# Fused attention and two expert layers: q and k of seven head pairs read by feature, key sums all on TensorE, a new written order

## The chip, the cores and the metric

The kernel runs on one core of a Trainium2 chip. The time is device microseconds (us) from the first to the last instruction of a launch, with what lies around it. Before the change the median of three runs is 609.99 us (609.46 to 610.15).

## The reference

Three layers follow one another; the change touches the first alone.

```
q_rot, k_rot = rotate(q), rotate(k)          # (2, 8, 576, 64): x1*cos - x2*sin | x1*sin + x2*cos
scores = (q_rot @ k_rot.T) / sqrt(64); scores -= max over keys
attn = exp(scores); attn /= sum over keys + 1e-9
x = attn @ v                                 # to (1152, 512)
x = leaky(x @ w_in) @ w_out                  # 512 -> 2048 -> 512
top-2 of 8 experts by noisy logits; out += gate * (relu(x @ w1[e]) @ w2[e])
```

All is computed to float32 accuracy: an operand of a product is cut into a rounded high part and a rest (low part), and a product is high·high + low·high + high·low, three TensorE passes at one pass each.

## The kernel before

Attention takes two heads (a pair) at a time, eight pairs in all, with the 576 tokens in five blocks of 128 columns (the last is half empty; the two heads share it). For each pair:

- **Loads.** SyncE's queue loads q and k by token (`load_qk`, L268: tokens on the partitions, 256 KB in rows of 1 KB and a rest of 32 KB in rows of 256 bytes) and v (`load_v`).
- **Rotation.** `rope` (L299) multiplies by cosine and sine tables and adds: four instructions for q and four for k, on VectorE for pair 0 (letter O of the order below), on GpSimd for pairs 1 to 7 (letter P).
- **Turning.** `turn` (L324; letters Q and K) makes TensorE transpose the rotated tokens into a PSUM tile, features on the partitions; ten small products for q and ten for k. The PSUM tile is one of three slots that the scores and the maxima use too.
- **High and low part.** ScalarE copies the turned tile, rounded, to `high` (`turn_high`, L349; h, i), VectorE subtracts it from the turned tile to `low` (`turn_low`, L354; j, n).
- **Maxima.** `max_scores` (M) makes plain products, VectorE reduces them (`max_reduce`, D), `max_turn` (R) and `max_rows` (m) bring the row maxima in place.
- **Scores.** `scores` (L411; S) makes a cell of 288 queries and 128 keys for both heads: four terms of two products, each product on 64 rows of TensorE's array. ScalarE takes the exponential from PSUM into `prob` (W).
- **Values and sums.** `values` (L426; V) multiplies `prob` with v on column strips of 32, four strips beside each other. `sums_of` (L444; G) multiplies with ones, in the same strips, to sum over keys. Before, key blocks 0 and 1 are added first by VectorE and blocks 2 and 3 by GpSimd (`add`, L439; + and ^), so a pair has three groups of sums: `GROUPS, ADDERS = ((0, 1), (2, 3), (4,)), ((0,), (1,))`.
- **Closing.** The sums go to DRAM and back spread over the partitions (t, T, s, B), GpSimd multiplies (N), ScalarE and GpSimd write the high and low part of x (X, Y).

What order the four compute engines and SyncE work in is written out by hand as a string `ORDER` (L508): one letter is one step, each engine takes its own steps in the string's order, and an engine that waits holds back all that stands behind it on that engine. Letter o is an idle product on TensorE; w, Z, F, l, k, c load; !, #, $, %, & and * are six steps that convert the first weights of the next layer.

`raw[pr % 2]` holds the loaded q and k of two pairs at a time. After attention the next layers run on TensorE without a gap; they aren't touched.

Of the kernel before, what the change touches and what calls it, by code (L numbers as in the profile page):

```python
# [16 lines left out]
OP = mybir.AluOpType  # L17
# [68 lines left out]
def fused_kernel(ctx, tc, q, k, v, w_in, w_out, w_gate, w_noise, noise, w1, w2, consts, out):  # L86
# [147 lines left out]
    GROUPS, ADDERS = ((0, 1), (2, 3), (4,)), ((0,), (1,))  # L234
# [12 lines left out]
    for i in range(2):  # L247
        raw.append({n: ap.tile([128, 2, KT, D], F32, name=f"raw_{n}{i}") for n in "qk"})
        VF.append(ap.tile([128, 2, 4, D], F32, name=f"VF{i}"))
        VT.append(ap.tile([128, 2, D], F32, name=f"VT{i}"))  # L250
        peak.append(ap.tile([128, KT, 65], F32R, name=f"peak{i}"))
        MR.append(ap.tile([128, KT * 128], F32R, name=f"MR{i}"))

    def fill(n):
        for t, v in ((raw[0]["q"][64:128, :, 4, :], 0.0), (raw[0]["k"][64:128, 0, 4, :], 0.0), (raw[0]["k"][0:64, 1, 4, :], 0.0),
                     (ones, 0.0), (ones[0:1, 0, :], 1.0), (ones[64:65, 0, :], 1.0), (ones[0:1, 1, 0:64], 1.0),
                     (ones[64:65, 1, 64:128], 1.0), (MR[0], 0.0), (peak[0], 0.0), 
                     (add_up[:, 0], 1.0), (add_up[0:64, 1], 1.0), (add_up[64:128, 1], 0.0), (add_up[0:64, 2], 0.0),
                     (add_up[64:128, 2], 1.0), (VT[0][64:128, 0], 0.0), (VT[0][0:64, 1], 0.0),
                     (raw[1]["q"][64:128, :, 4, :], 0.0), (raw[1]["k"][64:128, 0, 4, :], 0.0),  # L260
                     (raw[1]["k"][0:64, 1, 4, :], 0.0), (MR[1], 0.0), (peak[1], 0.0),
                     (VT[1][64:128, 0], 0.0), (VT[1][0:64, 1], 0.0))[FILLS[n][0]:FILLS[n][1]]:
            G.memset(f32(t) if t.dtype == F32R else t, v)

    FILLS = ((0, 8), (8, 10), (10, 17), (17, 24))

    def load_qk(pr, n, part, a=slice(0, 2), queue=None):

        b, h0 = divmod(pr, 4)
        h0 *= 2  # L270
        src, t = q if n == "q" else k, raw[pr % 2][n]
        base = src.offset + (b * H + h0 + a.start) * S * D
        heads = [S * D, a.stop - a.start]
        if part == 0:
            (queue or nc.sync).dma_start(t[:, a, 0:4, :].rearrange("p h j d -> p h (j d)"),
                                         bass.AP(tensor=src.tensor, offset=base, ap=[[4 * D, 128], heads, [1, 4 * D]]))
        else:
            r = 64 if n == "k" and a.start == 1 else 0
            (queue or nc.sync).dma_start(t[r:r + 64, a, 4, :],
                                         bass.AP(tensor=src.tensor, offset=base + 512 * D, ap=[[D, 64], heads, [1, D]]))  # L280
# [17 lines left out]
    def rope(pr, n, eng, i, a0=0, a1=2):  # L298
        x = raw[pr % 2][n]  # L299
        if (pr, n) not in roped:  # L300
            roped[pr, n] = [a2.tile([128, KT, 2, D], F32, name=m) for m in ("rope_" + n, "rope_t")]
        hs = slice(a0, a1)
        r, t = (y[:, :, hs] for y in roped[pr, n])
        rv, tv = (y.rearrange("p j h d -> p h j d") for y in (r, t))
        if (pr, n, i) == (1, "q", 0) and not FIRST_G:
            G.tensor_copy(hold, roped[0, "k"][0][0:1, 0, 1, 0:1])
# [16 lines left out]
    def turn(pr, n, a, at=None):  # L323


        r = roped[pr, n][0]
        if pr == 0:
            if at is None:
                p = aside.append(ps_o.tile([128, 1024], F32, name="pT", tag="o")) or aside[0]
            else:  # L330
                p = ps(at, "pT", (128, 1024))
            turned[pr, n, a] = p
            for j in range(KT):
                if a == 0:
                    T.transpose(p[:64, j * 128:(j + 1) * 128], r[:, j, 0], ident)
                else:
                    T.transpose(p[:, j * 128:(j + 1) * 128], r[:, j].rearrange("p h d -> p (h d)"), ident)
            return
        p = ps(at, "pT")
        for j in range(KT):  # L340
# [98 lines left out]
    def add(pr, g, z, eng):  # L439
        t = joined[pr, g, z] = a2.tile([128, 2, 288], F32, name=f"both{g}{z}", bufs=1)  # L440
        i, j = GROUPS[g]
        eng.tensor_tensor(t, prob[pr, i, z], prob[pr, j, z], op=OP.add)

    def sums_of(pr, g):  # L444

        y, js = acc[pr], GROUPS[g]
        for o in range(2):
            x = joined[pr, g, o] if len(js) == 2 else prob[pr, js[0], o]
            for a in range(2):
                for c in range(2):  # L450
                    T.matmul(y[64 * a + 32 * c:64 * a + 32 * c + 32, o, 288:432], add_up[:, 0 if js[0] < 4 else 1 + a],
                             x[:, a, c * 144:c * 144 + 144], start=False, stop=(g == len(GROUPS) - 1), skip_group_check=True)
# [56 lines left out]
"ckfcokcokkofokkokfokoooOoIoOfoOooOOQ0OlOoohOloOK1lOOoloiOoOlQ2OOlM0hOM1lDPKwjM0ioloDPM2woDM1lPoFDM0PoolDoooDoP"  # L509
"lQ2nR1whM0ooFPmojowS1PD!wM2oWwDPS0lM1WS2DPS0Wl+K1lWM2lViDPVF!nM0S2PDM1WPVDM2R0DM1mPlM0DS2ZDM1lWPDM0S2PDM1WVPDM"  # L510
"0S2DS1W^l+K0WlQ2M1hVDPVijVGn^M1S2DM0WVPJDR1PM2#mGGDPM0S1DM2WDS0PQ1$WS2hVPWVjM0wUPS2DwM1PWlDS0lM2WS1DPZK0+WtS2M"
"1WV+wVi^lVDlVnM2S1PDM0WVPDS2PJM1M0WDVVD^M2R1DM0mVDPM2S1DS0WTQ2PWsM1GDPhGVPjM0S1DM2PWDS0K1WM2GPDiVPnS0US2PM1WtV"
"DWV#lM0S1JDlS2W+S0lWS1+lWM2^wVDWlG!lM0R1PDM2lmVTlDS0PwS1$WsS2PWM0wVWBD^S1%S2WM0BVWPVDlM1S2DZS0PW+K1M2iVGNWnGVD"
"VPQ0UPM1S2DhPtVJVWjM1&wS2^DwS0W+ZR1WVPlmM2wS0DS1WTS2P%WM0VWPVDM1S2PDM0WVDM1NS2DM0WVD^Q1*K2hM0VXDGPiGjVXVnPM0wS"
"1PDM2FWGPDsS0UJF+M1S2wWVYZWVDtR0M2^M1mDVV!BDM0S2DlS1W+S0lW^M2VD&VWM1YS2DS0W#M1GWPDVM2S0DPS1W#Q2WPM0VDhGPVjM1S0"
"DNS2WTS1J+sWK0wWS2*i^VGWnwS1UB$S2M0!VwW%VZVWDtVX+VFM1M2R0DNwVmDZV&M1^S0DS2WTS1$sWYM0GXVWDS2S1+WS0BW+M2VW*GGDV#"
"S1%UM0S2DWtVNWV!M1M0M2^D&VVDXV^DVVTJ$VsYGFS1wS0*wWR2wW%GBVm#V$&GS1U*S0%S2WtWVWS1NS0WS2&YS1WTV+sWVFVW*V^+S0S2WB"
"S1W^GXFVVWYVGGVVNUXtY")
# [7 lines left out]
    first = [(0, n, i, slice(a, a + 1), x) for a, x in enumerate((nc.sync, nc.scalar)) for n in "qk" for i in range(2)]  # L526
# [3 lines left out]
    def idle():  # L530
# [12 lines left out]
            "O": (rope, [(0, n, V, i, a, a + 1) for n, a in FIRST_V for i in range(4)] +
                  [(pr, n, V, i) for pr, n in pairs[2:] if (pr, n) in ROPE_V for i in range(4)]),
            "P": (rope, [(0, n, G, i, a, a + 1) for n, a in FIRST_G for i in range(4)] +
                  [(pr, n, G, i) for pr, n in pairs[2:] if (pr, n) not in ROPE_V for i in range(4)]),
            "Q": (turn, [(0, "q", 0), (0, "q", 1)] + [(pr, "q", None) for pr in some]),
            "K": (turn, [(0, "k", 0), (0, "k", 1)] + [(pr, "k", None) for pr in some]),
# [16 lines left out]
    work["G"] = (sums_of, [(pr, g) for pr in range(NP) for g in range(len(GROUPS))])  # L565
# [825 lines left out]
```

## Time and profile before

| | |
|---|---|
| median of three runs | 609.99 us |
| the profiled execution | 609.47 us, its span 607.7 us |
| TensorE busy | 595.4 us, 98% |
| VectorE, ScalarE, GpSimd busy | 70%, 49%, 42% |
| attention, first instruction to the next layer's first product | 0 to 148.8 us |
| first score (S) of pair 0 | 17.23 us |
| granted clock | 0.998 |

The profile names engines PE (TensorE matrix products), PEld (its weight loads), DVE (VectorE), ACT (ScalarE), POOL (GpSimd) and SP (SyncE). Products follow one another before the one ahead has ended, so the step from one start to the next is what a product costs, and a busy PE may still be one that waits a little.

### The profile page before, as it was taken

The page shows a single profiled execution, that of the slowest core. Times are in us where ns is not written, and L with a number is a line of the kernel's source. Part 1 is how long each engine was busy: PE and PEld are TensorE (multiplying, and loading weights), DVE is VectorE, ACT ScalarE, POOL GpSimd, SP SyncE. Part 2 cuts the span into 40 slices and gives each one's busy share as a digit, 9 for nine tenths or more (in the row PEclk, how much of TensorE's full clock was granted, in tenths as well). Part 3 has the DMA queues.
Part 4 walks back from the last instruction along what each step waited for, and adds up shares of the span by engine and source line. Part 5 has one row for each costly group of instructions (what it writes and reads, how often), then busy time and mean ns, then how long its engine had stood idle before and what let it go on. Part 6 is the DMA issues. An engine that isn't in the chain of part 4 may idle for free. (4 is left out here: it accounts for less than half of the span.)

```text
span 607.7 us, 12491 instructions
## 1 busy us (share of the span) xinstructions
PE 595.4 (98%) x4736; PEld 501.4 (83%) x4737; DVE 427.3 (70%) x900; ACT 295.9 (49%) x604; POOL 254.3 (42%) x256
## 2 busy tenths in 40 slices
PE   8999999999999999999999999999999999999994
PEld 4666766777888888888999988888888888888883
DVE  7888887883898888833378667777676777776610
ACT  2554665756554544433234453454545455555411
POOL 6999799637300000100000204473838383838212
PEclk9999999999999999999999999999999999999999
DMA  6520323233357843650654431558585767676323
GB/s 194 157 54 24 109 54 112 78 86 102 97 147 264 274 139 109 222 174 2 207 171 140 151 100 48 192 178 220 155 211 180 188 189 196 181 204 181 77 39 45
DMA packets 83214, 85.84 MB, mean 141 GB/s; under 512 B 12365, under 2 KB 64973, under 8 KB 83150
## 3 DMA queue, kind: packets, MB, share of 16 engines
q1 hardware_dynamic: 76878, 73.82, 39.2%
q0 software_dynamic: 5392, 10.49, 9.1%
q8 instruction: 38, 0.62, 0.4%
q10 hardware_dynamic: 880, 0.69, 0.4%
q14 instruction: 26, 0.21, 0.1%
HBM read 69.96 MB, written 14.98 MB: 140 GB/s over the span
## 5 line engine op out<-in xcount | busy, mean ns | idle before, releaser
L968 POOL DMA_INDIRECT got<-x_rows,chunks x70 | 81.6, 1166 | 78.9 <-ACT wh L217 45.3
L219 DVE TENSOR_TENSOR wl<-raw,wh 128x512 fp32r<-128x512 f32 x128 | 82.6, 683 | 14.8 <-ACT wh L217 14.7
L599 PE MATMUL bank<-xe_h,wl 128*128 128x320 f32 x248 | 76.8, 310 | 0.0
L599 PE MATMUL bank<-xe_l,wh 128*128 128x320 f32 x248 | 76.8, 310 | 0.0
L599 PE MATMUL bank<-xe_h,wh 128*128 128x320 f32 x248 | 76.7, 309 | 0.0
L217 ACT ACTIVATE wh<-raw 128x512 fp32r<-128x512 f32 x128 | 74.2, 627 | 0.0
L620 ACT ACTIVATE g_t<-bank 128x512 f32<-128x512 f32 (+2 forms) x48 | 23.6, 492 | 94.8 <-PE bank L599 93.8
L422 ACT ACTIVATE p<-pS 128x576 f32<-128x576 f32 x80 | 49.1, 651 | 40.1 <-PE pS L418 39.0
L1160 PE MATMUL bank<-wh,g_x 128*128 128x512 f32 x192 | 68.0, 395 | 0.0
L608 PE MATMUL bank<-g_h,wh 128*128 128x512 f32 (+2 forms) x192 | 65.1, 339 | 0.0
L599 PE MATMUL bank<-xh,wh 128*128 128x512 f32 (+2 forms) x192 | 65.0, 338 | 0.0
L599 PE MATMUL bank<-xh,wl 128*128 128x512 f32 (+2 forms) x192 | 64.9, 338 | 0.0
L608 PE MATMUL bank<-g_l,wh 128*128 128x512 f32 (+2 forms) x192 | 64.7, 337 | 0.0
L599 PE MATMUL bank<-xl,wh 128*128 128x512 f32 (+2 forms) x192 | 64.7, 337 | 0.0
L608 PE MATMUL bank<-g_h,wl 128*128 128x512 f32 (+2 forms) x192 | 64.5, 336 | 0.0
L381 DVE TENSOR_REDUCE half<-pM 128x2 f32<-128x640 f32 x70 | 51.5, 754 | 16.1 <-PE pM L369 15.6
L621 DVE TENSOR_TENSOR g_f<-bank,g_t 128x512 f32<-128x512 f32 (+2 forms) x48 | 26.7, 557 | 45.4 <-ACT g_t L620 44.9
L1186 POOL DMA_INDIRECT out<-y_row,idx x24 | 39.9, 1663 | 35.7 <-ACT y_row L1171 17.9
L1141 ACT ACTIVATE g_x<-bank 128x320 fp32r<-128x320 f32 x48 | 21.0, 438 | 63.0 <-PE bank L599 59.3
L599 PEld LDWEIGHTS bank<-xe_h,wh 128*128 128x128 f32 x248 | 46.7, 188 | 5.8
L1143 DVE SCALAR_TENSOR_TENSOR g_x<-bank,g_x 128x320 fp32r<-128x320 f32 x48 | 23.4, 488 | 36.5 <-ACT g_x L1142 36.5
L599 PEld LDWEIGHTS bank<-xe_h,wl 128*128 128x128 f32 x248 | 46.6, 188 | 2.8
(250 smaller groups left out, 1436.0 us busy)
## 6 DMA issues: line engine op xcount, KB each, us to landing
raw<-in_moe_w SPq DMA_DIRECT2D x128, 256.0 KB
raw<-in_moe_w_in SPq DMA_DIRECT2D x16, 512.0 KB
raw<-in_moe_w_out SPq DMA_DIRECT2D x16, 512.0 KB
inv_sum<-inv_sums SPq DMA_DIRECT2D x16, 144.0 KB
out<-none SPq DMA_DIRECT2D x9, 256.0 KB
VF<-in_v SPq DMA_DIRECT2D x8, 256.0 KB
kept<-wh SPq DMA_DIRECT2D x4, 512.0 KB
kept<-wl SPq DMA_DIRECT2D x4, 512.0 KB
```

Source lines behind the costliest of these rows:

```text
L217: A.activation(hi[:, part], t, AF.Copy)
L219: V.tensor_tensor(lo[:, part], t, f32(hi)[:, part], op=OP.subtract)
L381: V.tensor_reduce(halves[pr, i][:, :, j], p[:, :, :(320, 256)[i]], axis=AX.X, op=OP.max, negate=True)
L422: A.activation(t, scored.pop((pr, j, z))[:, :, 0:288], AF.Exp, scale=0.125)
L599: T.matmul(h[:, :n], w[:, 0, k * 128:(k + 1) * 128], m[:, k, cols:cols + n], start=(i == 0), stop=(i == 11))
L608: T.matmul(b[:, o:o + n], w[:, 1, ds], m[:, :n], start=(first and opens and t == 0), stop=(last and t == 2), skip_group_check=True)
L620: A.activation(t[:, :n], h[:, :n], AF.Copy, scale=0.01)
L621: V.tensor_tensor(g[:, :n], h[:, :n], t[:, :n], op=OP.max)
L968: G.indirect_dma_start(out=got[e][:, b * 128:(b + 1) * 128], out_offset=None, in_=x1_rows.rearrange("n (q c) -> (n q) c", q=4), in_offset= ...
L1143: V.scalar_tensor_tensor(g[:, C:2 * C], h[:, :C], 0.0, f32(g)[:, :C], op0=OP.max, op1=OP.subtract)
L1160: T.matmul(yr[st], s, w, start=(f == 0 and t == 0), stop=(f == 7 and t == 2))
L1186: s = G.indirect_dma_start(out=out, out_offset=bass.IndirectOffsetOnAxis(ap=idx[e][:r.shape[0], st:st + 1], axis=0), in_=r, in_offset=None ...
```

## The change

- For pairs 1 to 7, q and k come from a new array `heads` that is laid out before the launch: features of both heads on the 128 partitions, tokens along the columns, once as they are and once with the two halves of the features swapped, with zeros in the empty columns. A load is 640 KB in rows of 5 KB (128 partitions x 1280 numbers). `angles` (2 x 320 KB) holds the cosines and the signed sines in the same layout.
- GpSimd rotates in place with three instructions of 640 columns for q and three for k (two products, one sum). There is no turning for these pairs: `high` and `low` are taken from `raw` in SBUF.
- Pair 0 is loaded, rotated and turned as before.
- GpSimd's additions of key blocks 2 and 3 go; TensorE sums each of these blocks by itself, four groups for a pair. The order of a pair's groups is set by `SUMS`.
- `ORDER` is another string. In it 140 of 160 turning products are gone (18 steps Q and K become 4), the 16 steps ^ are gone, G has 32 steps for 24, P 42 for 56, o 31 for 35, l 14 for 35; the other counts are the same.

```diff
+def angles():
+    ...
+    c = np.stack([np.concatenate([cos[s], cos[s]], 1), np.concatenate([-sin[s], sin[s]], 1)]).transpose(2, 0, 1)
+    return np.ascontiguousarray(np.concatenate([c, c]))
+def heads(q, k):
+    out = np.zeros((2, B * H // 2 - 1, 2, D, 2, KT * 128), np.float32)
+    for i, x in enumerate((q, k)):
+        x = np.asarray(x).reshape(B * H // 2, 2, S, D)[1:].transpose(0, 1, 3, 2)
+        for w, y in enumerate((x, np.roll(x, D // 2, axis=2))):
+            ...
-    GROUPS, ADDERS = ((0, 1), (2, 3), (4,)), ((0,), (1,))
+    GROUPS, ADDERS = ((0, 1), (2,), (3,), (4,)), ((0,), ())
+    SUMS = [(i // 4, int(g)) for i, g in enumerate("10231023012310230123102310231023")]
...
-        raw.append({n: ap.tile([128, 2, KT, D], F32, name=f"raw_{n}{i}") for n in "qk"})
+        raw.append({n: ap.tile([128, 2, KT * 128], F32, name=f"raw_{n}{i}") for n in "qk"})
+    angle = ap.tile([128, 2, KT * 128], F32, name="angle")
...
+    def load_turned(pr, n):
+        nc.sync.dma_start(raw[pr % 2][n].rearrange("p w n -> p (w n)"), heads["qk".index(n), pr - 1].rearrange("p w n -> p (w n)"))
+    def load_angle(i):
+        nc.sync.dma_start(angle[:, i], angles[:, i])
...
+    def rope_turned(pr, n, i):
+        x = raw[pr % 2][n]
+        if (pr, n, i) == (1, "q", 0) and not FIRST_G:
+            G.tensor_copy(hold, roped["k"][0][0:1, 0, 1, 0:1])
+        if i < 2:
+            G.tensor_tensor(x[:, i], x[:, i], angle[:, i], op=OP.mult)
+        else:
+            G.tensor_tensor(x[:, 0], x[:, 0], x[:, 1], op=OP.add)
...
-        for j in range(KT):
-            for w in range(2):
-                T.transpose(p[:, w, j * 64:(j + 1) * 64], r[here(w), j].rearrange("p h d -> p (h d)"), ident[here(w), here(w)])
+    def source(pr, n, a=1):
+        return raw[pr % 2][n][:, 0] if pr else turned[n, a][:, :KT * 128]
     def turn_high(pr, n, a):
-        ...
+        A.activation(high[n][pr % NSET][here(a)], source(pr, n, a)[here(a)], AF.Copy)
     def turn_low(pr, n):
-        ...
+        V.tensor_tensor(low[n][pr % NSET], source(pr, n), f32(high[n][pr % NSET]), op=OP.subtract)
...
     ORDER = (
-"ckfcokcokkofokkokfokoooOoIoOfoOooOOQ0OlOoohOloOK1lOOoloiOoOlQ2OOlM0hOM1lDPKwjM0ioloDPM2woDM1lPoFDM0PoolDoooDoP"
-"lQ2nR1whM0ooFPmojowS1PD!wM2oWwDPS0lM1WS2DPS0Wl+K1lWM2lViDPVF!nM0S2PDM1WPVDM2R0DM1mPlM0DS2ZDM1lWPDM0S2PDM1WVPDM"
...
+"ckfkokcokkookkoceokoloeoOoooOoOoOooOIQ0OfOoOohOfK1OOoofiOwoOQ2wOOM0whOM1DlKZPDM0iooFDM1ZDM0PZoDM1ZoDwM0PowjR1o"
+"womnooPloDS2FM1lWS0PDM2WS1DS0WPM2hVDVW+VPiS1M2M0WDR1PDM2mDM0S1PDM2WVDS0jPM1M2WS0DVWlPDZhM1M0VZDGPDM2S1DS0WJVi+"
...
```

## Rows read from the trace of the kernel before

**Rows 1.** The page's first part: busy us, share of the span, instructions.

```profile
PE 595.4 (98%) x4736; PEld 501.4 (83%) x4737; DVE 427.3 (70%) x900; ACT 295.9 (49%) x604; POOL 254.3 (42%) x256
```

**Rows 2.** Busy time by stretch: stretch, length, then each engine, clock, DMA share, GB/s.

```profile
0.00:17.20 17.20, 15.14 (x84) 7.97 (x85) 12.14 (x30) 5.23 (x9) 12.07 (x37) 1.00 0.69 197
17.20:83.20 66.00, 64.15 (x954) 45.12 (x955) 56.74 (x77) 37.53 (x60) 60.48 (x48) 1.00 0.29 80
83.20:148.80 65.60, 65.33 (x1067) 45.65 (x1063) 49.53 (x72) 40.18 (x68) 45.94 (x35) 1.00 0.32 89
```

**Rows 3.** TensorE's timeline, 102 to 108 us: start, length, line, tiles, count.

```profile
103.90 0.70 PE L451 MATMUL pO<-both,add_up 128*32 128x144 f32 x16
104.41 0.67 PE L435 MATMUL pO<-p,VF 128*32 128x288 f32 x8
105.01 0.39 PE L369 MATMUL pM<-high_k,high_q 64*128 64x256 f32 x2
105.23 0.30 PE L418 MATMUL pS<-high_q,high_k 64*128 64x288 f32 x2
...
106.30 0.51 PE L342 MATMUL pT<-ct,rope_q 64*128 64x64 f32 x10
106.67 0.41 PE L369 MATMUL pM<-high_k,high_q 64*128 64x320 f32 x2
```

**Rows 4.** GpSimd's timeline, 28 to 39 us.

```profile
28.79 1.56 POOL L313 TENSOR_TENSOR rope_k<-rope_k,rope_t 128x640 f32<-128x640 f32 x1
30.30 2.01 POOL L442 TENSOR_TENSOR both<-p 128x576 f32<-128x576 f32 x1
...
37.13 1.56 POOL L313 TENSOR_TENSOR rope_q<-rope_q,rope_t 128x640 f32<-128x640 f32 x1
```

**Rows 5.** TensorE's timeline, 38 to 43 us, with idle time and who ended it.

```profile
38.98 0.47 PE L342 MATMUL pT<-ct,rope_q 64*128 64x64 f32 x10
39.26 0.38 PE L418 MATMUL pS<-high_q,high_k 64*128 64x288 f32 x2
...
42.56 0.41 PE L369 MATMUL pM<-high_k,high_q 64*128 64x320 f32 x2 [0.58 <-DVE low_q L356]
```

**Rows 6.** VectorE's timeline from the first maximum to the first score.

```profile
10.35 0.76 DVE L376 TENSOR_REDUCE peak<-pM 128x1 fp32r<-128x576 f32 x1
11.03 0.81 DVE L356 TENSOR_TENSOR low_q<-pT,high_q 128x640 fp32r<-128x640 f32 x1
11.76 3.45 DVE L376 TENSOR_REDUCE peak<-pM 128x1 fp32r<-128x576 f32 x5
15.61 0.82 DVE L356 TENSOR_TENSOR low_k<-pT,high_k 128x640 fp32r<-128x640 f32 x1 [0.39 <-PE pT L532]
```

**Rows 7.** TensorE's timeline, the same stretch.

```profile
15.49 0.52 PE L342 MATMUL pT<-ct,rope_q 64*128 64x64 f32 x10
15.82 0.34 PE L396 MATMUL pR<-ident_r,peak 64*65 64x64 f32 x6
...
17.23 0.40 PE L418 MATMUL pS<-high_q,high_k 64*128 64x288 f32 x2
```

**Rows 8.** Line 442 and line 356: count, duration ns min/median/max, first and last start.

```profile
L442 DVE TENSOR_TENSOR both<-p x16: 686/752/2106, 20.3 to 142.1; 128x576 f32<-128x576 f32 x16
...
L356 DVE TENSOR_TENSOR low_q<-pT,high_q x8: 808/815/825, 11.0 to 107.9; 128x640 fp32r<-128x640 f32 x8
```

**Rows 9.** GpSimd's groups, 0 to 148 us: count, busy us, mean ns, idle before.

```profile
L442 POOL TENSOR_TENSOR both<-p 128x576 f32<-128x576 f32 x16 | 24.2, 1520 | 6.2 <-ACT p L422 6.2
L311 POOL TENSOR_TENSOR rope_t<-raw_q,ct_att 128x320 f32<-128x320 f32 x14 | 12.6, 917 | 0.0
L308 POOL TENSOR_TENSOR rope_q<-raw_q,ct_att 128x640 f32<-128x640 f32 x7 | 10.9, 1555 | 0.1
```

**Rows 10.** VectorE's additions of line 442, as groups, 0 to 148 us.

```profile
L442 DVE TENSOR_TENSOR both<-p 128x576 f32<-128x576 f32 x16 | 16.4, 1033 | 0.2 <-ACT p L422 0.2
```

**Rows 11.** Busy time by stretch, 10 to 15 us, columns as in rows 2.

```profile
10.00:15.00 5.00, 4.67 (x25) 2.77 (x25) 5.00 (x8) 1.22 (x2) 4.43 (x5) 1.00 0.86 253
```

More of the change, by code (lines that the diff above doesn't have):

```diff
@@ L78, in constants @@
     return c
+def angles():
+    half = D // 2
+    inv_freq = 1.0 / 10000.0 ** (np.arange(0, half, dtype=np.float32) / half)
+    freqs = np.outer(np.arange(S, dtype=np.float32), inv_freq)
+    cos, sin = np.cos(freqs).astype(np.float32), np.sin(freqs).astype(np.float32)
+    s = np.concatenate([(4 * np.arange(128)[None] + np.arange(4)[:, None]).reshape(-1), 512 + np.arange(128) % 64])
+    c = np.stack([np.concatenate([cos[s], cos[s]], 1), np.concatenate([-sin[s], sin[s]], 1)]).transpose(2, 0, 1)
[5 more added lines that the diff above has]
+        for w, y in enumerate((x, np.roll(x, D // 2, axis=2))):
+            out[i, :, :, :, w, :512] = y[..., :512].reshape(*y.shape[:3], 128, 4).swapaxes(3, 4).reshape(*y.shape[:3], 512)
+            for a in range(2):
+                o = 512 + 64 * a * i
+                out[i, :, a, :, w, o:o + 64] = y[:, a, :, 512:]
+    return out.reshape(2, B * H // 2 - 1, 128, 2, KT * 128)
 def f32(t):
@@ L85, in fused_kernel @@
 @with_exitstack
-def fused_kernel(ctx, tc, q, k, v, w_in, w_out, w_gate, w_noise, noise, w1, w2, consts, out):
+def fused_kernel(ctx, tc, q, k, v, w_in, w_out, w_gate, w_noise, noise, w1, w2, consts, heads, angles, out):
     nc = tc.nc
@@ L296, in fused_kernel, with rope @@
     roped = {}
[L298 to L301, printed above, removed]
+    def rope(n, eng, i, a0, a1):
+        x = first_raw[n]
+        if n not in roped:
+            roped[n] = [a2.tile([128, KT, 2, D], F32, name="rope_" + n, bufs=1), a2.tile([128, KT, 2, D], F32, name="rope_t")]
         hs = slice(a0, a1)
-        r, t = (y[:, :, hs] for y in roped[pr, n])
+        r, t = (y[:, :, hs] for y in roped[n])
         rv, tv = (y.rearrange("p j h d -> p h j d") for y in (r, t))
-        if (pr, n, i) == (1, "q", 0) and not FIRST_G:
-            G.tensor_copy(hold, roped[0, "k"][0][0:1, 0, 1, 0:1])
         if i == 0:
@@ L321, in here, with turn @@
         return slice(0, 128) if a is None else slice(64 * a, 64 * a + 64)
[L323 to L329, printed above, removed]
-            else:
-                p = ps(at, "pT", (128, 1024))
-            turned[pr, n, a] = p
-            for j in range(KT):
[L334 to L340, printed above, removed]
-            for w in range(2):
-                T.transpose(p[:, w, j * 64:(j + 1) * 64], r[here(w), j].rearrange("p h d -> p (h d)"), ident[here(w), here(w)])
-        turned[pr, n, a] = p[:, :, :KT * 64].rearrange("p w (j n) -> p j w n", n=64)
-    def like(pr, t):
-        return t if pr == 0 else t.rearrange("p (j w n) -> p j w n", j=KT, w=2)
+    def turn(n, a, at=None):
+        r = roped[n][0]
+        if at is None:
+            p = aside.append(ps_o.tile([128, 1024], F32, name="pT", tag="o")) or aside[0]
+        else:
+            p = ps(at, "pT", (128, 1024))
+        turned[n, a] = p
+        for j in range(KT):
+            if a == 0:
+                T.transpose(p[:64, j * 128:(j + 1) * 128], r[:, j, 0], ident)
+            else:
+                T.transpose(p[:, j * 128:(j + 1) * 128], r[:, j].rearrange("p h d -> p (h d)"), ident)
+    def source(pr, n, a=1):
+        return raw[pr % 2][n][:, 0] if pr else turned[n, a][:, :KT * 128]
     def turn_high(pr, n, a):
-        x = turned[pr, n, a]
-        t = high[n][pr % NSET][here(a)]
-        A.activation(like(pr, t), x[here(a), :KT * 128] if pr == 0 else x, AF.Copy)
+        A.activation(high[n][pr % NSET][here(a)], source(pr, n, a)[here(a)], AF.Copy)
     def turn_low(pr, n):
-        x = turned[pr, n, None if pr else 1]
-        V.tensor_tensor(like(pr, low[n][pr % NSET]), x[:, :KT * 128] if pr == 0 else x, like(pr, f32(high[n][pr % NSET])),
-                        op=OP.subtract)
+        V.tensor_tensor(low[n][pr % NSET], source(pr, n), f32(high[n][pr % NSET]), op=OP.subtract)
     maxed, halves = {}, {}
@@ L439, in add @@
     def add(pr, g, z, eng):
-        t = joined[pr, g, z] = a2.tile([128, 2, 288], F32, name=f"both{g}{z}", bufs=1)
+        t = joined[pr, g, z] = a2.tile([128, 2, 288], F32, name=f"both{z}")
         i, j = GROUPS[g]
@@ L525, in fused_kernel @@
     both = [(0, n, a) for n in "qk" for a in range(2)]
-    first = [(0, n, i, slice(a, a + 1), x) for a, x in enumerate((nc.sync, nc.scalar)) for n in "qk" for i in range(2)]
+    first = [(n, i, slice(a, a + 1), x) for a, x in enumerate((nc.sync, nc.scalar)) for n in "qk" for i in range(2)]
     spare = ps_o.tile([128, 2, 512], F32, name="pW", tag="o")
@@ L538, in fused_kernel @@
             "k": (load_qk, first),
-            "l": (load_qk, [(pr, n, i, s) for pr, n in pairs[2:] for i, s in
-                            [(0, slice(0, 2))] + ([(1, slice(0, 2))] if n == "q" else [(1, slice(a, a + 1)) for a in range(2)])]),
+            "l": (load_turned, pairs[2:]), "e": (load_angle, [(0,), (1,)]),
             "f": (fill, [(i,) for i in range(len(FILLS))]),
             "I": (lambda: G.tensor_copy(ident_r, ident), [()]),
[L543 to L548, printed above, removed]
+            "O": (rope, [(n, V, i, a, a + 1) for n, a in FIRST_V for i in range(4)]),
+            "P": (rope_turned, [(pr, n, i) for pr, n in pairs[2:] for i in range(3)]),
+            "Q": (turn, [("q", 0), ("q", 1)]), "K": (turn, [("k", 0), ("k", 1)]),
             "w": (load_v, [(pr, i) for pr in range(NP) for i in range(3)]),
@@ L564, in fused_kernel @@
         work[n] = (add, [(pr, g, z, (V, G)[i]) for pr in range(NP) for g in ADDERS[i] for z in range(2)])
-    work["G"] = (sums_of, [(pr, g) for pr in range(NP) for g in range(len(GROUPS))])
+    work["G"] = (sums_of, SUMS)
     work["J"] = (max_join, [(pr,) for pr in some])
@@ L1377 @@
     arrays, args = {}, []
+    made = {"constants": constants(), "heads": heads(inputs["q"], inputs["k"]), "angles": angles()}
     dealt = {"moe_w_out": 1, "moe2_w_gate": 0, "moe2_w_noise": 0, "moe2_w1": 1}
-    for name in _INS + ["constants"]:
-        a = constants() if name == "constants" else np.ascontiguousarray(inputs[name])
+    for name in _INS + list(made):
+        a = made[name] if name in made else np.ascontiguousarray(inputs[name])
         if name in dealt:
```

43 lines of the change are left out of this document (20 added, 23 removed).

## The prediction

> **What bounds the kernel now.** I read the page's engine line first: TensorE is busy 595 of 607.7 us and nothing else is over 70% [rows 1]. So the time is TensorE's, and a change counts only where it takes work from TensorE's queue or lets a late step start earlier. All the change's edits lie in attention, the first 148.8 us of the span; the 459 us after it go on without a gap, whatever their own pace, and I move them as a block.
>
> Then the busy time by stretch, cut at the first score (17.23 us) and the middle of attention (83.2 us, the 41st score) [rows 2]. TensorE looks full in both halves, but its ends are modelled, so I count its work by steps from one start to the next [rows 3]: two cells of scores take 1.07 us, 0.535 each; a group of sums 0.51; a cell of values 0.60 where other work follows and about 0.51 where it doesn't (it streams as many columns as a group of sums); a maximum 0.22; a turn 0.37. I take a turn of the row maxima at 0.30, below a turn. Counted in the old order, the half from 17.2 to 83.2 us has 40 scores (21.4), 45 maxima (9.9), 33 values at 0.55 (18.2), 9 sums (4.6), 9 turns (3.3), 5 turns of row maxima (1.5): 58.9 us of work in 66.0. The half behind it has 40 scores, 28 maxima, 47 values, 15 sums, 4 turns, 3 of row maxima: 63.5 in 65.6. So TensorE loses about 7 us in the first half, 2 in the second.
>
> What ends these waits is seen in the timelines. In the first half GpSimd is busy 60.5 of 66 us, VectorE 56.7 [rows 2]. GpSimd finishes pair 3's q at 38.69 [rows 4]; its turn starts at 38.98, VectorE makes the low part after it, and TensorE stands 0.58 us before the maximum at 42.56 for that low part [rows 5]. So in the first half GpSimd's rotation, put off by additions standing among it (30.30) [rows 4], paces the pairs.
>
> **The change part by part.**
>
> *Turning.* Seven pairs lose two turns each: 14 x 0.37 = 5.2 us off TensorE. Below, 0.28, what one took at 38.98 until the next score [rows 5]: 3.9. The upper end is the 0.37.
>
> *Sums.* Eight pairs have four groups for three: 8 x 0.51 = 4.1 us more [rows 3]; no turn was hidden and no sum will be, both are in TensorE's own queue.
>
> *Excursions to the strips of 32 columns.* Counting runs of values and sums in both strings gives 42 before, 44 after; leaving costs 0.60 - 0.51 = 0.09 [rows 3], entering I take as much again: 2 x 0.18 = 0.4. Scores and maxima alternate 54 times for 59; I cost that at nothing.
>
> Together TensorE has 5.2 - 4.1 - 0.4 = 0.7 us less, between 0.6 more (turn at 0.28) and 0.9 less. By halves, with the counts of the new string: 40 scores, 43 maxima, 35 values, 12 sums, 5 row maxima make 57.8 in the first (58.9 before), 40, 30, 45, 20 and 3 make 63.9 in the second (63.5). This agrees: -0.7.
>
> *The opening.* VectorE's first maximum starts at 10.35; among the six it now makes a low part (11.03), and the second low part waits 0.39 for idle products and ends at 16.43 [rows 6]. The turn of row maxima stands behind pair 1's turn (15.49) and comes at 15.82, the first score at 17.23 [rows 7]. In the new string the six maxima run straight (10.35 + 0.76 + 5 x 0.69 = 14.5), the turn of row maxima follows them without another pair's turn ahead, and the two low parts (1.63) end near 16.1. First score near 16.2: 1.0 us earlier. The other end: angles and the larger loads. By 10.6 us GpSimd needs one table of 0.33 MB and 0.66 MB of q where it needed 0.29 MB: 0.7 MB more, at the 253 GB/s that a busy stretch shows [rows 11] 2.8 us, part of it in gaps (the first 17 us use 69% of the DMA engines [rows 2]). Pair 1 isn't wanted by TensorE until over 20 us, so I let this cost nothing; if it delays pair 0's own loads it costs up to 1.5. Later loads (0.66 MB at 253 GB/s: 2.6 us, twice a pair of about 16 us) have room where DMA stands at 29% [rows 2]; each must wait for the low part of the pair two before, and SyncE's queue holds v loads and the sums' round trip behind it. Both have a pair's time to spare.
>
> *GpSimd.* Its 16 additions go (24.2 us [rows 9]); a rotation is 3 x 1.56 = 4.7 for 1.56 + 2 x 0.92 + 1.56 = 5.0. In the first half that is 26 steps P (40 us) and little else, 43 of 66 us for 60.5. Pair 3's q could be ready near 34 for 38.7 us. With no turn, TensorE and its PSUM slot also drop out of the path to the low part. What is late next is VectorE.
>
> *High and low part.* ScalarE reads SBUF instead of PSUM; the trace has it busy 57% of the first half [rows 2], so a tenth of a microsecond each way hides. VectorE's low part read one operand from PSUM: 0.815 us, never over 0.825 while GpSimd worked [rows 8]. Now both are in SBUF. The nearest rows are VectorE's own additions of two SBUF operands, 576 columns: 0.69 to 2.11 [rows 8], mean 1.03 [rows 10]. For 640 columns: 0.77 to 2.3, I take 1.15: 0.33 more, between 0.05 less and 1.5 more. Nine such low parts fall in the first half: +3.0 on VectorE. With three maxima fewer and three more conversion steps it stands near 59 to 60 of 66, up to 70 at the upper end.
>
> The Trainium skill, "SBUF — State Buffer", section "Who interferes with whom", says that a VectorE instruction with two SBUF inputs and a GpSimd instruction that reads SBUF exclude each other for a whole instruction. The spread of [rows 8] fits it: the PSUM form is even, the SBUF form isn't. By that rule a low part would wait on average half a rotation (0.78) in the share of time that GpSimd works (43 of 66), 0.5 each, 4.5 us for nine: VectorE at 61 of 66 us, and the sum below the same; that the waits fall worse than their average is the first rival.
>
> *Waits.* In the first half neither TensorE (57.8) nor VectorE (60) nor GpSimd (43) fills 66 us. I let 1.1 of the 7 us lost there go: GpSimd's pacing falls away, VectorE's gets tighter. Ends: 5 us less, 4 more.
>
> Sum: -0.7 - 1.0 - 1.1 = -2.8. Against the profiled execution, 609.47 (span 607.7 and 1.8 around it), that is 606.7; the median of the runs shown is 0.5 higher, so 607.2.
>
> **The rivals.** *VectorE becomes the bound.* Low parts meet GpSimd's rotations, which now run without a pause, and take 1.8 us, 1.0 more each. It decides from the point where the first half's idle time of VectorE, 66 - 56.7 = 9.3 us [rows 2], is used up: nine low parts eat 9.0, and the waits for TensorE that made that idle time don't all vanish, some 4 us of the half come on top. 609.99 - 0.7 - 1.0 + 4 = 612.3. For it: in the opening VectorE is already full (5.00 of 5 [rows 11]) and an addition took 2.11 [rows 8]. Against: GpSimd works a third less, so VectorE's additions and conversions gain. The rule of the Trainium skill named above ("SBUF — State Buffer") is this rival's mechanism.
>
> *Work only.* The opening gains nothing because larger loads come late, and the waits keep their size: 609.99 - 0.7 = 609.3. For it: 86% of the DMA engines' time in use at 10 to 15 us [rows 11]. The same time comes out if it does less than it says, the turns removed and the sums added cancelling.
>
> *The waits mostly go.* With GpSimd no pacer and slots freed by 14 turns, 4 of 7 us vanish: -0.7 - 1.0 - 4 = -5.7, 604.3. Against: VectorE was at 86%.
>
> **How the numbers follow.** The forecast has 0.45 (its own range 606.0 to 608.7), VectorE as the bound 0.20 (610.5 to 614), work only 0.20 (608.5 to 610.2), waits gone 0.15 (603.5 to 606). A measurement here tells 0.2%, 1.2 us, from no change, so faster is below 608.8: nearly all of the first (0.43), the fourth (0.15), a little of the third (0.04): 0.62. Same (to 611.2): 0.20, the third and the edges. Slower: 0.18. I leave out the ends of both sides, one in ten each: 604.0 to 611.8.
>
> **What would show it.** Right: first score before 16.5 us; attention's last product near 146 us; no idle time of TensorE put down to GpSimd; a group of sums still 0.51 from start to start; low parts between 0.77 and 2.3, mean near 1.15. Wrong: a mean over 1.6 and TensorE's waits ended by low_q or low_k before the 41st score (the first rival); the first score at or after 17.2 with VectorE waiting for a DMA (work only). It would also be wrong if the 459 us behind attention changed their length.

## The result and the profile after

The changed kernel takes 614.57 us (median of six runs, 611.01 to 617.5) against 609.85 for the kernel before on the same chip: ratio 1.0078, 95% interval 1.0061 to 1.0096. It is slower by 4.7 us, where 2.8 us faster was forecast; the time lies outside the range given. The profiled execution took 614.72 us, its span 612.7 (607.7 before), at a mean granted clock of 0.992. The page's engine line answers to [rows 1]:

```profile
PE 594.6 (97%) x4720; PEld 501.8 (82%) x4721; DVE 427.9 (70%) x900; ACT 295.4 (48%) x604; POOL 231.2 (38%) x223
```

TensorE's busy time fell by 0.8 us and GpSimd's by 23; all that the change was to take away is gone. The span still grew by 5.0. I cut it at two starts that both traces have, the first score of pair 0 and the first product behind attention:

| us | before | after | difference |
|---|---|---|---|
| start to first score | 17.23 | 21.75 | +4.52 |
| first score to end of attention | 131.56 | 132.24 | +0.68 |
| all behind attention | 458.9 | 458.7 | -0.2 |

So nearly everything is lost before the first score. Theory C of the expectations below, that the steady part makes the loss (low parts from SBUF, four groups of sums), has at most the 0.68 us of the second row. The busy time by stretch (stretch, length, then PE, PEld, DVE, ACT, POOL, granted clock, DMA share, GB/s) shows what the opening of the changed kernel looks like; the halves below it answer to [rows 2]:

```profile
5.00:10.00 5.00, 2.03 (x8) 0.64 (x6) 3.53 (x10) 0.00 (x0) 0.00 (x0) 1.00 0.96 313
10.00:15.00 5.00, 4.60 (x31) 3.50 (x31) 2.61 (x6) 2.38 (x4) 4.28 (x16) 1.00 1.04 320
15.00:20.00 5.00, 4.12 (x23) 2.15 (x22) 4.01 (x7) 0.91 (x2) 4.92 (x5) 0.92 0.89 302
20.00:25.00 5.00, 4.29 (x27) 3.41 (x28) 2.37 (x4) 1.08 (x2) 4.92 (x5) 0.50 0.28 110
...
21.70:88.00 66.30, 63.57 (x924) 44.76 (x925) 55.95 (x76) 36.97 (x60) 46.22 (x28) 0.97 0.36 111
88.00:154.00 66.00, 64.93 (x1095) 46.55 (x1091) 49.01 (x72) 40.96 (x70) 36.44 (x25) 1.00 0.37 108
```

The same stretch of the kernel before:

```profile
5.00:10.00 5.00, 4.60 (x28) 2.53 (x26) 4.59 (x15) 1.57 (x3) 2.21 (x8) 1.00 0.63 175
```

From 5 to 10 us the DMA engines go from 63% to 96% busy, and at the same time ScalarE and GpSimd do nothing at all and TensorE loses more than half of its work. Full transfer and idle engines side by side mean that the engines wait for data, and for other data than what is being moved. VectorE's timeline of the changed kernel (start, length, line, tiles; in brackets the idle time before it and who ended it) says which:

```profile
8.59 0.49 DVE L343 TENSOR_TENSOR rope_q<-rope_q,rope_t 128x320 f32<-128x320 f32 x1
10.81 0.49 DVE L338 TENSOR_TENSOR rope_k<-raw_k,ct_att 128x320 f32<-128x320 f32 x1 [1.72 <-DMA raw_k<-in_k]
...
18.51 0.81 DVE L384 TENSOR_TENSOR low_q<-pT,high_q 128x640 fp32r<-128x640 f32 x1
19.83 0.82 DVE L384 TENSOR_TENSOR low_k<-pT,high_k 128x640 fp32r<-128x640 f32 x1 [0.51 <-PE pT L559]
```

The rotation of the k of pair 0's second head starts at 10.81, after a wait for its load; before, VectorE started on it at 8.88 without a wait. Its two loads (128 and 16 KB, on ScalarE's queue) were issued at 3.58 and 5.54 us, before at 4.19 and 5.24, so the larger one was issued earlier and still landed later. The line of before:

```profile
8.88 0.48 DVE L308 TENSOR_TENSOR rope_k<-raw_k,ct_att 128x320 f32<-128x320 f32 x1
```

The identity, which TensorE needs for every turn, is late too. GpSimd's cast of it, its first instruction in the stretch, shows when it landed. GpSimd's timeline after, then before:

```profile
10.39 0.29 POOL L568 CAST ident_r<-ct 128x128 fp32r<-128x128 f32 x1 [8.03 <-DMA ct<-in_constants]
```

```profile
5.34 0.61 POOL L542 CAST ident_r<-ct 128x128 fp32r<-128x128 f32 x1 [1.12 <-DMA ct<-in_constants]
```

TensorE's timeline of the changed kernel answers to [rows 7]:

```profile
10.40 0.71 PE L373 MATMUL pT<-ct,rope_q 128*64 128x128 f32 x5 [3.37 <-DMA ct<-in_constants]
...
13.21 0.78 PE L396 MATMUL pM<-high_k,high_q 64*128 64x320 f32 x4
...
18.74 0.36 PE L423 MATMUL pR<-ident_r,peak 64*65 64x64 f32 x6
19.03 0.69 PE L559 MATMUL pT<-warm 128*128 128x384 bf16 x2
20.71 1.12 PE L559 MATMUL pT<-warm 128*128 128x384 bf16 x3 [0.98 <-DVE low_k L384]
21.75 0.61 PE L445 MATMUL pS<-high_q,high_k 64*128 64x288 f32 x2
22.16 0.44 PE L445 MATMUL pS<-low_q,high_k 64*128 64x288 f32 x2
22.40 0.44 PE L445 MATMUL pS<-high_q,low_k 64*128 64x288 f32 x2
```

Three losses can be read here. The first turn stands 3.37 us for the identity (10.40 for 5.86). The three idle products at 20.71, which write the same tile of PSUM (the memory that takes TensorE's products) as the turned k, wait 0.98 for the low part that reads it, and then stand in front of the score. And from 19 us on everything runs at half pace: two products of a score step by 0.24 us where they step by 0.13 later. The granted clock is 0.50 from 20 to 25 us, the lower of the two levels (1.2 of 2.4 GHz), after TensorE had first stood 3.4 us and then had small gaps among the maxima.

### The profile page after: what moved, and what is told of

Its sections match the earlier page's. It is cut to its first block, busy times and chain, and to the rows that moved or that the text cites. A ratio compares the mean times of both kernels' runs of the same rounds, so it can differ in the third digit from the quotient of the medians.

```text
span 612.7 us, 12414 instructions
## 1 busy us (share of the span) xinstructions
PE 594.6 (97%) x4720; PEld 501.8 (82%) x4721; DVE 427.9 (70%) x900; ACT 295.4 (48%) x604; POOL 231.2 (38%) x223
## 5 line engine op out<-in xcount | busy, mean ns | idle before, releaser
L245 DVE TENSOR_TENSOR wl<-raw,wh 128x512 fp32r<-128x512 f32 x128 | 82.6, 683 | 14.8 <-ACT wh L243 14.7
```

Of the source, the lines that this page charges most:

```text
L245: V.tensor_tensor(lo[:, part], t, f32(hi)[:, part], op=OP.subtract)
```

## The experiments

Theory B was that the three large loads of the opening (angles and pair 1's q, 1.28 MB) take the DMA engines from pair 0's k and the identity. Theory A, its rival, was that only the identity's own load hurts, since its letter (the third c) stands further back in the new string: the load is issued at 3.99 us for 1.72. Ratios are to the kernel before, run on the same chip.

**e1: the identity's load early, nothing else.**

```diff
-"ckfkokcokkookkoceokoloeo...
+"ckfkokccokkookkoeokoloeo...
```

> The changed kernel with one letter moved: the identity table's load stands on ScalarE's queue ahead of the second head's q and k again, as before the change. Theory A (the identity, landed at 10.4 us in the changed kernel, sets the start of TensorE's work; its queue place is the cause): identity lands near 5.5 us, first turn near 6 us, first score 18 to 19 us for 21.75, clock not halved, time 3 us or more shorter, near 611.5. Theory B (the 640 KB and 320 KB loads crowd out all of pair 0's loads, so the second head's k still comes at 10.8 us): first turn early, but first score not before 20 us, at most 1.5 us shorter, 613 to 614. Theory C (the loss is in the steady part, low parts from SBUF and four groups of sums): within 1 us of the changed kernel.

614.96 us, ratio 1.005 (1.0028 to 1.0072). The cast comes at 5.32 and the first turn at 7.09, but the second head's k still comes at 11.24, and the first score at 23.13, later still, with the clock at half from 13 to 26 us. (The profiled execution, 619.07 us, is the longest of the eight.) A falls: with the identity early, the rest of the opening is as late as in the changed kernel.

**e2: the large loads held, the identity as it was.** Their letters (e, l, e) go behind pair 0's first turn, and GpSimd first writes one number into each of the three tiles, behind the identity's cast, so that the loads can't start earlier.

```diff
+  (angle[0:1, 0, 0:1], 0.0), (angle[0:1, 1, 0:1], 0.0), (raw[1]["q"][0:1, 0, 0:1], 0.0),
-"...kkookkoceokoloeoOooo...IQ0OfOoO...
+"...kkookkocokoooOooo...IQ0OfeleOoO...
```

> The changed kernel with the two angle tables and pair 1's first load held back until GpSimd has cast the identity table (three one-element fills of their tiles come first); the identity's place in ScalarE's queue stays late. Theory A: the identity is still issued third, lands about 6.5 us, first score 18 to 19, time near 611. Theory B: all of pair 0's loads land by 8 us, first score near 17, time 4 to 5 us shorter, 609.5 to 610.5; pair 1's rotation then starts some 2 us later than in the kernel before, which TensorE doesn't need before 22 us. Theory C: within 1 us of the changed kernel.

611.57 us, ratio 0.999 (0.9974 to 1.0006). The second head's k is back at 8.96, the identity lands by 6.81 though its letter stands late, and the first score is at 18.70. B holds: held loads alone give back 3.05 of the 4.52 us. It isn't the whole: B had the first score near 17.

**e3: both edits.**

> Both edits together. Theories A and B: first score 16.2 to 17, clock full throughout, time 5 us or more under the changed kernel, 608 to 609.5, so at or a little under the kernel before. Theory C: still 3 us or more over the kernel before.

610.04 us, ratio 0.9979 (0.9963 to 0.9996). The cast is at 5.47, the k at 8.90, yet the first score at 18.76 is no earlier than in e2, where 16.2 to 17 at full clock was expected. So the place of the identity's letter is worth nothing here. TensorE's timeline of e3 shows what is left:

```profile
15.44 0.54 PE L424 MATMUL pR<-ident_r,peak 64*65 64x64 f32 x6
15.91 0.82 PE L560 MATMUL pT<-warm 128*128 128x384 bf16 x2
17.71 1.12 PE L560 MATMUL pT<-warm 128*128 128x384 bf16 x3 [0.99 <-DVE low_k L385]
18.76 0.61 PE L446 MATMUL pS<-high_q,high_k 64*128 64x288 f32 x2
```

The idle products still wait for low_k and still stand ahead of the score, and they still run at half clock (0.51 from 15 to 20 us), now without the long stop: only the gaps among the maxima came before.

**e4: only the stop filled.** In the changed kernel, with its early loads, 13 more idle products stand ahead of the first turn.

```diff
-"...OooOIQ0OfO...
+"...OooOIoooooooooooooQ0OfO...
```

> The changed kernel with 13 more idle products ahead of the first turn, about 3.6 us of them, in the time in which TensorE stood still (7.0 to 10.4 us); no load is moved. If the halved clock from 19.5 to 25.9 us comes from this gap, the granted clock stays at full, the first score comes near 21 and the time is about 2 us shorter, 612 to 612.5. If it comes from the small gaps between 15 and 21 us, the clock falls all the same and the time stays. By no theory does the first turn start before 10.4.

613.13 us, ratio 1.003 (1.0005 to 1.0056). The first turn is still at 10.42, but TensorE stands only 1.37 us before it and the clock stays at its upper level:

```profile
15.00:20.00 5.00, 3.95 (x23) 2.11 (x22) 4.19 (x7) 0.94 (x2) 4.92 (x4) 1.00 0.95 276
20.00:25.00 5.00, 4.45 (x49) 3.49 (x52) 3.00 (x5) 2.42 (x4) 4.92 (x5) 1.00 0.42 170
```

The first score comes 0.62 earlier (21.13) and pair 0's stretch is 0.98 shorter (18.29 for 19.27). So the fall of the clock costs 1.6 us; the loads cost the greater part. (Attention ends 2.7 us earlier in all, at 151.28; the part behind it took 460.0 us here for 458.7, for a reason that isn't known.)

**e5: e3, and idle products moved** from behind the row maxima, where they waited for low_k, to places before it: four go there, seven come among the maxima and behind the turn of the row maxima, so there are three more in all.

```diff
-...ZDM0PZoDM1ZoDwM0PowjR1o"
-"womnooPloDS2...
+...ZDM0PZoooDM1ZooDwM0PooowjR1ooo"
+"wmnPlDS2...
```

> e3_both with idle products moved only: none any more between pair 0's last low part and the first score, four more among the maxima and three behind the turn of row maxima, ahead of the low part that waits for their tile. In e3_both they held back the low part by 0.9 us and the first score by 1.1 more, at half clock. Expected if the rest of the opening's loss is the place of the idle products and the clock: first score 16.6 to 17.2 for 18.8, clock full, time 2 to 3 us under e3_both, so 607 to 608 where the kernel before has 610. If the clock falls all the same (TensorE stands about 0.8 us before the first score): first score near 17.5, 609.

608.54 us, ratio 0.998 (0.997 to 0.9989): 0.2% faster than the kernel before. By ratio that is no more than e3 had (0.9979), where 2 to 3 us less was expected. The profiled executions differ by 1.8 us (spans 609.3 and 607.5), but on two chips. TensorE's timeline:

```profile
15.71 0.36 PE L424 MATMUL pR<-ident_r,peak 64*65 64x64 f32 x6
16.01 0.66 PE L560 MATMUL pT<-warm 128*128 128x384 bf16 x3
16.60 0.40 PE L446 MATMUL pS<-high_q,high_k 64*128 64x288 f32 x2
16.84 0.29 PE L446 MATMUL pS<-low_q,high_k 64*128 64x288 f32 x2
17.66 0.40 PE L446 MATMUL pS<-high_q,low_k 64*128 64x288 f32 x2 [0.52 <-DVE low_k L385]
```

The first score is at 16.60 at full clock, 2.16 earlier than in e3, and it starts before the low part of k is there; its third term waits 0.52 us for that. So what the 2.16 us are worth for the whole time isn't shown.

**e8: e5's move of idle products in the changed kernel, loads left early.**

> The changed kernel with the idle products moved as in e5_idle_moved and nothing else; loads and identity late as in the changed kernel. If the place of the idle products is a loss of its own, on top of the late loads: first score near 20 us for 21.75, 1 to 3 us under the changed kernel, 611 to 613. If the late loads make the whole loss: first score 21 to 22 and 614 as before.

615.02 us, ratio 1.0078 (1.0052 to 1.0104), as the changed kernel. First score at 21.16. Without the held loads the better place of the idle products is worth nothing that the whole time shows. In the profile attention ends at 152.12, 1.9 us earlier, but the clock fell at another place (10 to 13 us), and the part behind attention took 460.3 us for 458.7.

**e9: e5 once more.**

> The kernel of e5_idle_moved once more, not edited: identity early, the three large loads held until VectorE has pair 0's work, idle products moved from behind the row maxima to between the maxima. If its gain of 0.2% over the kernel before is one of the kernel and not of one chip and hour, the ratio comes out at 0.998 again (0.9965 to 0.9995), first score 16.5 to 17.7, granted clock over 0.99 from 15 to 20 us. If the gain was chance, the ratio is 1.000 or above.

609.32 us, ratio 0.998 (0.9971 to 0.9989), first score 17.34. The gain of 0.2% is repeated.

Then the two parts of the change apart, in the order string of before.

**d1: the sums alone.** GpSimd's additions go, each of its groups becomes two on TensorE.

```diff
-    GROUPS, ADDERS = ((0, 1), (2, 3), (4,)), ((0,), (1,))
+    GROUPS, ADDERS = ((0, 1), (2,), (3,), (4,)), ((0,), ())
-"0S2DS1W^l+K0WlQ2M1hVDPVijVGn^M1S2...
+"0S2DS1Wl+K0WlQ2M1hVDPVijVGnGGM1S2...
```

> The kernel before, in its own order, with one part of the change alone: GpSimd's additions of key blocks 2 and 3 dropped, TensorE sums each block (the two new groups stand where GpSimd's second addition stood). By the price of the forecast, 0.51 us a group, TensorE has 4.1 us more: 3 to 4.5 us slower than before, with the opening and the clock unchanged (first score near 17.2). If GpSimd's additions were what paced the first half, less: 0 to 2 us slower.

615.47 us, ratio 1.0095 (1.0081 to 1.011). First score 17.55; from there to the end of attention 137.38, 5.8 more than before, where eight groups were priced at 4.1 and 3 to 4.5 was expected.

**d2: the layout alone, loads ahead of the low parts.** Each load of the pair after next stood ahead of the low part that still reads the tile, so low parts read another pair's numbers.

> The kernel before, in its own order, with the other part alone: q and k of pairs 1 to 7 by feature, no turning; GpSimd's additions stay. Angles and pair 1's first load stand where pair 1's loads stood. Theory A+B (the loss is the opening, where large loads compete with pair 0's): the identity lands in time, the second head's k late (10 to 11 us for 8.9), first score 19 us or later, clock halved for some us; behind the first score shorter than before by about the turns, 3 to 5 us; in all within 2 us of the kernel before. Theory C (low parts from SBUF cost the steady part): from the first score to the end of attention not shorter than the 131.6 us of before.

628.18 us, ratio 1.0294. The opening's loads weren't held here (second head's k at 11.45, first score 23.22), and the waits aren't those of the change; nothing is concluded from it but the opening once more.

**d3: the layout alone**, opening loads held, loads behind the low parts, GpSimd's additions kept.

> The kernel before in its own order with the new layout alone, as d2_layout_alone was meant: GpSimd's additions stay, turns of pairs 1 to 7 dropped, three steps P for four. Loads of pairs 3 to 7 stand behind the low parts of the pair two before (in d2_layout_alone they stood ahead of them, so low parts waited for the wrong pair's load and took its data), and angles and pair 1's first load are held until the identity is cast. If a turn is worth the 0.28 to 0.37 us of the forecast: first score 16.5 to 17.5, from there to attention's end 126 to 128 us for 131.6, in all 3 to 5 us under the kernel before. If GpSimd and the low parts' lock take it back: 130 to 133 and within 1 us of the kernel before.

620.3 us, ratio 1.0153 (1.0134 to 1.0171). First score 17.70, but 143.05 from there to the end, 11.5 more than before, where at most 133 was expected. Line 385, the low parts (duration ns min/median/max), and one stretch of d3:

```profile
L385 DVE TENSOR_TENSOR low_q<-raw_q,high_q x7: 812/1446/2152, 16.8 to 119.6; 128x640 fp32r<-128x640 f32 x7
L385 DVE TENSOR_TENSOR low_k<-raw_k,high_k x7: 1264/1681/2169, 24.3 to 123.9; 128x640 fp32r<-128x640 f32 x7
```

```profile
20.00:45.00 25.00, 19.89 (x266) 13.12 (x266) 22.74 (x26) 12.63 (x21) 24.69 (x15) 1.00 0.44 137
```

The same line (384) of the changed kernel, and its VectorE additions as a group:

```profile
L384 DVE TENSOR_TENSOR low_q<-raw_q,high_q x7: 753/815/1397, 32.6 to 137.3; 128x640 fp32r<-128x640 f32 x7
L384 DVE TENSOR_TENSOR low_k<-raw_k,high_k x7: 807/818/2176, 39.7 to 136.6; 128x640 fp32r<-128x640 f32 x7
```

```profile
L469 DVE TENSOR_TENSOR both<-p 128x576 f32<-128x576 f32 x16 | 13.4, 842 | 0.0
```

With GpSimd at 24.69 of 25 us, VectorE's low parts take twice as long and TensorE falls to 19.89 of 25: the first rival, as forecast, but in a kernel that keeps the additions. TensorE waits 2.25, 2.81 and 2.06 us for VectorE's maxima at 39.23, 48.88 and 105.03 us, and its clock falls too (0.52 from 48 to 50 us, 0.50 to 52, 0.82 to 60, and 0.91 from 100 to 120). That is some 10 us at the lower level in all, so by estimate up to 5 of the 11.5 us are the clock's. In the changed kernel GpSimd is free enough that it doesn't happen on the whole. Alone, in the order of before, the parts are 0.95% and 1.53% slower; together, with the new order and a mended opening, 0.2% faster. How much of that difference the two parts make together and how much the new order makes, no run separates.

**e6 and e7: the wait in the middle.** TensorE's longest wait behind the first score in the changed kernel is at 91.50 us. VectorE's, GpSimd's and TensorE's timelines there:

```profile
86.73 1.94 DVE L233 SCALAR_TENSOR_TENSOR word<-raw,word 128x512 int32<-128x512 int32 x1
88.59 2.12 DVE L469 TENSOR_TENSOR both<-p 128x576 f32<-128x576 f32 x1
90.63 2.74 DVE L408 TENSOR_REDUCE half<-pM 128x2 f32<-128x640 f32 x4
```

```profile
86.27 3.82 POOL L350 TENSOR_TENSOR raw_q<-raw_q,angle 128x640 f32<-128x640 f32 x2 [1.20 <-DMA raw_q<-in_heads]
90.17 1.94 POOL L352 TENSOR_TENSOR raw_q<-raw_q 128x640 f32<-128x640 f32 x1
```

```profile
91.50 0.38 PE L396 MATMUL pM<-high_k,high_q 64*128 64x256 f32 x2 [1.07 <-DVE half L408]
```

Two VectorE instructions with both inputs in SBUF, 0.7 and 0.75 us elsewhere, take 1.94 and 2.12 beside the rotation, and GpSimd's two products 3.82 for 3.02. If this meeting is what costs, moving the weight conversion ($) out of it should help. e6 is e5 with $ later, e7 with $ earlier:

```diff
-...VJ#WVnV...S0$WNV...XDGGDVDPM1...
+...VJ#WVnV...S0WNV...XDGGDVDP$M1...     (e6)
+...VJ#$WVnV...S0WNV...XDGGDVDPM1...     (e7)
```

> e5_idle_moved with one conversion step of VectorE ($, two instructions) put behind seven maxima in the middle of attention, where the changed kernel's VectorE met GpSimd's rotation three times in a row (1.94 and 2.12 us for 0.69 and 0.75) and TensorE stood 1.1 us for a maximum. If the lock between the two engines made that wait: the wait is gone, 1 to 1.5 us less in the runs in which e5_idle_moved has it, equal in those in which it hasn't. If the wait had another cause: no difference.

> e5_idle_moved with the same conversion step ($) put earlier, ahead of four low parts, where GpSimd stood idle some 4 us; e6_conversion_later put it behind the maxima and there it met the next rotations (three more waits of 1.3 to 1.8 us). If the lock makes the wait of TensorE at the 41st to 50th score: that stretch 20 us for 21.2, 1 to 1.3 us under e5_idle_moved. If not: as e5_idle_moved, or longer where the low parts come late for the 41st score.

e6: 615.22 us, ratio 1.0067 (1.0041 to 1.0093); e7: 611.34, 0.9999 (0.9985 to 1.0014). Neither helps. In e7 the rotation meets the conversion at 81.92 and an addition at 83.90 instead, and TensorE waits 1.35 us at 86.81. In VectorE's timeline of e7:

```profile
81.92 2.06 DVE L235 SCALAR_TENSOR_TENSOR word<-raw,word 128x512 int32<-128x512 int32 x1
83.90 2.12 DVE L470 TENSOR_TENSOR both<-p 128x576 f32<-128x576 f32 x1
```

In e6 (the profiled execution is the longest of six) GpSimd's rotation stood 5.78 us before it started, TensorE waited 3.2 us for maxima and had the lower clock level from 92 to 95 and from 106 to 112 us; that pair took 28.06 us for 21.19. In both orders something else met the rotation (in e6, among others, two additions that took 4.15 us together at 100.07). That the meeting makes the wait fits e7, where both come earlier; since no order without the meeting was run, it isn't shown.

## Why the prediction was wrong

**The opening, the step that failed.** The prediction had the first score at 16.2 us, 1.0 earlier; it came at 21.75, 4.5 later. It did count 0.7 MB more to be moved early, 2.8 us of transfer, let it cost nothing since "Pair 1 isn't wanted by TensorE until over 20 us", and bounded the other case at 1.5 us. That zero is what failed: it asked when the new data is wanted, not what waits behind it. By the forecast's own rows, 69 to 86% of the DMA engines' time was in use before [rows 2, 11]; the loads don't pass beside pair 0's but among them. e2 shows that 3.05 us go to this alone, twice the bound. The prediction did name the sign (the first score at or after 17.2 with VectorE waiting for a DMA), but its rival "work only" let that cost no more than the 1.0 us not gained. It missed one thing more: the idle products, which the prediction mentions only as what the low part waits for, write the PSUM tile that low_k reads. They wait for it, and the score stands behind them. The identity's letter had moved too, which a count of letters doesn't show, but by e1 and e3 that cost the first score nothing.

Where idle products and loads are put right (e5), the first score comes at 16.60, in e9 at 17.34. That it comes near 16.2 is in part luck. The forecast had the six maxima end at 14.5 and both low parts near 16.1. VectorE's timeline of e5:

```profile
12.96 2.13 DVE L404 TENSOR_REDUCE peak<-pM 128x1 fp32r<-128x576 f32 x3 [0.50 <-PE pM L397]
16.78 0.82 DVE L385 TENSOR_TENSOR low_k<-pT,high_k 128x640 fp32r<-128x640 f32 x1 [0.95 <-PE pT L560]
```

The maxima wait for TensorE's products and end at 15.09; low_k waits for idle products and ends at 17.60. The score's third term, which needs it, starts at 17.66 (18.39 in e9), and the kernel before had it no later, by TensorE's timeline:

```profile
17.60 0.29 PE L418 MATMUL pS<-high_q,low_k 64*128 64x288 f32 x2
```

So the 1.0 us of the forecast was not seen in any run, even with the opening mended.

**The clock.** No rival had it. 1.6 us of the loss (e4) is TensorE at its lower level from 19 to 26 us. Of the 4.52 us before the first score that leaves 0.85 beside the loads (3.05) and the clock (0.62), if the two add; no run separates it.

**TensorE's work, -0.7.** The direction holds, the size isn't isolated. TensorE's busy time fell by 0.8 us over the span. From the first score to the end of attention it is the first number behind the comma, before and in e5:

```profile
17.23:148.79 131.56, 129.44 (x2017) 90.75 (x2016) 106.25 (x148) 77.68 (x128) 106.39 (x82) 1.00 0.30 85
16.60:148.66 132.06, 127.28 (x2014) 89.77 (x2013) 105.82 (x149) 77.89 (x130) 85.05 (x54) 1.00 0.39 123
```

In four variants of the changed kernel that were at full clock there (e4, e5, e8, e9) it is 126.7 to 127.3, so 2.2 to 2.8 us less than before. Since the ends of products are modelled, part of this can be short waits that count as busy before. A group of sums still steps by 0.5 us (0.52 and 0.49 at 91.81 and 92.33).

**The waits, -1.1.** Wrong in direction by the same rows: what isn't busy grows from 2.1 us before to 3.5 to 4.8 in these four (3.8 in the changed kernel). The 7 us that the forecast counted as lost in the first half were for the most part no idle time that the trace shows: 64.15 of 66.00 us are busy there [rows 2]. The forecast for first score to end was 129.8; it took 132.24, of that 0.98 by the clock, and at full clock 130.15 (e4), 130.96 (e8), 131.25 (e9) and 132.06 (e5). GpSimd did become free as forecast (46.2 of 66.3 us in the first half, 43 forecast), and no wait of TensorE's behind the first score is ended by it. But the wait at 91.50 came in its place: the fifth pair takes 21.21 us for 19.40 before; in e4, where no wait of TensorE's falls in that pair, 19.89.

**GpSimd's pace.** Pair 3's q was to be ready near 34 us. Its rotation starts at 37.49, after a wait of 4.50 us for its load:

```profile
37.49 3.68 POOL L350 TENSOR_TENSOR raw_q<-raw_q,angle 128x640 f32<-128x640 f32 x2 [4.50 <-DMA raw_q<-in_heads]
```

The load may start only when pair 1's low part of q (at 32.6 us) has read the tile. That the loads have "a pair's time to spare" was wrong: the rotation in place makes the loads the pacer. It ends no wait of TensorE's here.

**The low parts.** The right size: 1.05 us on average (14.7 us for fourteen) where 1.15 was taken, and VectorE at 55.95 of 66.3 us in the first half where 59 to 60 was forecast; its additions, for one, fell from 1033 [rows 10] to 842 ns. The Trainium skill, "SBUF — State Buffer", section "Who interferes with whom", has VectorE's instructions with two SBUF inputs and GpSimd's that read SBUF exclude each other. The traces agree, with 0.82 us alone and up to 2.18 beside a rotation, and in d3 with medians of 1.45 and 1.68. The lock weighs in d3; in the changed kernel it fits the place of one wait, and it didn't make the kernel slower as a whole.

What stays open: which of TensorE's gaps bring the clock down. e3 lost it without the long stop, e4 kept it with the gaps among the maxima unchanged, e8 lost it at 10 us, behind a stop of 2.46 us, and had it back by 14. Open too is where the 0.2% of e3, e5 and e9 comes from: in the profile of e5 attention ends at 148.66 us, 0.1 before the 148.79 of the kernel before. And the part behind attention took 460.0 to 460.3 us in the profiles of e4, e7 and e8, 458.6 to 459.0 in the others; why isn't known.

## What to carry to other kernels

An early load costs by what it shares the DMA engines with, not by when it is wanted: look which small transfers are in flight when a large one is added, and hold the large one until those have landed. Count what an order string moves, not only what it adds and drops, above all the loads and the idle products, and check what tile an idle product writes and who still reads it. Two edits that relieve and load the same two engines can't be judged by each alone: here each alone, in the old order, cost 0.95 to 1.5%, and both, with a new order and the opening mended, gained 0.2%. And time lost by a count of steps isn't yet a wait that can go: look whether the trace shows it as idle.

## What the runs showed of the hardware that wasn't expected

- Some 1.3 MB of loads in rows of 2.5 and 5 KB, issued among small ones, delayed the 64 KB of the identity, issued at 3.99 us, to 10.4 (by 6.81 with the loads held, e2; 5.32 issued ahead of them, e1), and the k of pair 0's second head by 1.9 us, while the DMA engines moved 313 GB/s.
- In d3 a low part of 0.82 us takes 1.45 to 1.68 us in the median beside a GpSimd that rests little (24.69 of 25 us busy from 20 to 45); GpSimd's products grow by 0.4 us each in such a meeting (3.82 for 3.02 the two).
- Thirteen idle products in front of the first turn kept TensorE at its upper clock level for all of the opening (e4), though the turn itself came no earlier.
